# Attention and a gated FFN on one core: first sums of w_out in the upper half of g_3, the last stage's PSUM tile in two, its loads in another order

## The chip, the cores and the metric

One core of a Trainium2 chip runs the whole program. The metric is device microseconds of one execution: the median of 3 runs before is 824.8 us (823.79 to 825.0). Engines: TensorE (PE) multiplies, VectorE (DVE) and ScalarE (ACT) work elementwise, GpSimd (POOL) adds and issues some DMAs, SyncE (SP) issues the other DMAs in the order of its queue. Each engine runs its own instructions in order and waits on counts of the others.

## The reference

```python
scores = scale * np.matmul(q_c, k_c.transpose(0, 1, 2, 4, 3))      # chunks of 64 tokens, 8 x 8 heads, float32
scores = scores - np.max(scores, axis=-1, keepdims=True)
attn = np.exp(scores); attn = attn / (np.sum(attn, axis=-1, keepdims=True) + 1e-09)
out = np.matmul(attn, v_c)
x = out as (4608 tokens, 512)
h = x @ w_in                                                       # 512 x 2048
g = h * (1.0 / (1.0 + np.exp(-1.702 * h)))
return (g @ w_out).astype(np.float32)                              # 2048 x 512
```

## The kernel before

Every float32 factor is split into a high and a low part that TensorE takes at full rate, and a product is three matmuls: high times low, high times high, low times high. The 4608 tokens are 9 blocks of 512. Blocks 0 to 2 are computed plainly. Blocks 3 to 8 go in three pairs (s = 0, 1, 2): `x @ w_in` of a pair is done for eight pairs p of slices of the hidden dimension, each by seven products P1, P2, P6, P7, P5, P3, P4 (i = 0 to 6, `product`, L858 to L860) of sums of quarters of x and of w_in, in place of eight. DVE and ACT drain the seven product banks (`drain`, L839 and L871) into four words per p.

The stage that matters here is the last pair, s = 2, and its `g @ w_out`, which `plan_last` also does by seven products, in the order P4, P1, P2, P6, P7, P5, P3 (L1101 to L1112, PSUM tiles `pl` and `att_last`). Its steps that the change touches:

- **Sums of w_out.** For each p, `plan_tsum` lets POOL add the high and low part of two slices of w_out (`whole`, L991, two instructions) and form four differences (L996 to L999). ACT makes the high part (`th`, L1003), DVE the low part in place (L1006), SP writes both to DRAM (`tsum`, L1010: touth, toutl). The sums alternate between two buffers: even p in `t_a` (tag sA, which later holds the words `kept_6`), odd p in `t_raw`. Sums p may overwrite a buffer only when toutl of p - 2 has landed.
- **x of the last pair.** `plan_x` subtracts quarters of x (L695) and writes high and low parts (L703 on ACT, L706 on DVE). Attention output of the tile pairs 28, 30, 32 and 34 is staged as `xs` in sA, in the half `xe3b` of the tile `g_3`, and in two temporary tiles. `g_3` is 4 x 512 words per partition; `xe3b` is its upper half. The last of these conversions reads the seventh difference, which stands in the second 512 words of `xe3b`.
- **PSUM.** Banks are four `po`, two `hp` and two of the tile `att_last` (L1167: one tile of 2 x 512). In the last pair the products of p take the banks of `turn` in rotation, att0 and att1 among them. Here each of these products and its drain wait on counts that the recording layer derives from the tiles they touch.
- **Loads.** `t_load` (L1063) brings the sums back: those of P4 into a ring of six pieces (the ring that `seven` loads of w_in sums used before), of P6 into w_8 to w_11, of P7 into w_12 to w_15, all through SP.

Which instruction comes when is set by `Plan`: steps with needs, takes, gives and a rank. `ORDER` lists the order by name up to the middle of the second pair; after it, a step goes when its engine is free, its needs are met and its rank is lowest; `NUDGE` shifts single ranks. The plan sets only the order in each queue. On the chip an instruction starts when its counts are reached.

Of the kernel before, what the change touches and what calls it, by code (L numbers as in the profile page):

```python
# [313 lines left out]
def tile_chunk_attention_ffn(  # L314
# [14 lines left out]
    P = 128  # L329
# [42 lines left out]
    }  # L372
    SHIFT = {10: 3.5, 8: 2.0, 26: -12.5, 12: 4.0, 34: -12.5, 6: 3.0}
# [4 lines left out]
    more = ctx.enter_context(tc.tile_pool(name="more", bufs=NTMP))  # L378
    ps_o = ctx.enter_context(tc.tile_pool(name="ps_o", bufs=1, space=bass.MemoryType.PSUM))
    ps_h = ctx.enter_context(tc.tile_pool(name="ps_h", bufs=2, space=bass.MemoryType.PSUM))  # L380
    ps_a = ctx.enter_context(tc.tile_pool(name="ps_a", bufs=1, space=bass.MemoryType.PSUM))

    ident = const.tile([P, P + 96], F32, tag="ident", name="ident")[:, :P]
    make_identity(nc, ident)
# [443 lines left out]
    def plan_two(s, p):  # L828
# [20 lines left out]
        def product(k, i):  # L849
            if bank(i) == "hp":  # L850
                hp = ps_h.tile([P, BT], F32, tag="hp", name=f"hp_{s}_{p}_{i}")
            else:
                hp = held["att"][:, int(bank(i)[3])] if bank(i)[0] == "a" else ps_o.tile([P, DM], F32, tag=bank(i), name=f"hp_{s}_{p}_{i}")
            st[i] = hp
            w = piece(k).rearrange("p (w c f) -> p w c f", w=2, c=2)
            xh, xl = [x_two(OPERANDS[names[i]][1], hl) for hl in range(2)]
            for c in range(2):
                nc.tensor.matmul(hp, w[:, 0, c], xl[:, c], start=c == 0, stop=False)  # L858
                nc.tensor.matmul(hp, w[:, 0, c], xh[:, c], start=False, stop=False)  # L859
                nc.tensor.matmul(hp, w[:, 1, c], xh[:, c], start=False, stop=c == 1)  # L860
# [51 lines left out]
        for i, name in enumerate(names):  # L912
            k = (7 * (NF // 2 * s + p) + i) % 6
            at = rank + STEP * i / 7
            plan.bulk(0.72, at - LEAD, lambda k=k, i=i: load(k, i), need=[f"po_{p}"], make=e(f"ld{i}"), take=[f"piece{k}"])
            xneed = [f"l{OPERANDS[name][1]}x_{s}_{h}" for h in range(2)] if p == 0 else []
            if final and i == 1 and p == 0:
                xneed.append(f"xs_{NTL - 1}")
            before = e(names[i - 1]) if i else h_event(START[s] - 1) if p == 0 else f"{names[6]}_{s}_{p - 1}"
            plan.add(  # L920
                PE, 1.36, at - 0.2, lambda k=k, i=i: product(k, i), need=[e(f"ld{i}"), before] + xneed, make=e(name),
                take=[bank(i)], give=[f"piece{k}"],
            )
            need, take = [e(name)], []
            if i in (1, 2, 3):
                need += [e("d0")] if i == 1 else [e(f"d{i - 1}")]
            if i == 4:
                need += [e("d3")]
                if end:
                    take = ["tmp"]  # L930
                elif final and p == NF // 2 - 1:
                    need += [f"l{x}x_{s}_{h}" for x in range(7) for h in range(2)]
                elif s:
                    need += [f"gl_{g1 - 2 * NF + h}" for h in range(2)]
                else:
                    need += [f"gal_{p // 2}"] + ([f"{x}_0_{h}" for x in ("l6x", "l3x", "t2x", "l5x", "t4x") for h in range(2)] if p > 3 else [])
            if i == 5:
                need += [e("d4")]
            if i == 6:
                need += [e("d4")]  # L940
            if i in (0, 3):
                take = ["tmp"]
            if final and i in (1, 6):
                need += [f"kept_{p}"]
            plan.add(
                ACT if i == 0 else DVE, 0.58 if i == 0 else 1.38 if i == 4 else 0.69, rank - 6 + 0.1 * i, lambda i=i: drain(i),
                need=need, make=e(f"d{i}"), take=take, give=[bank(i)] + ["tmp"] * (final and i in (4, 6)),
            )
# [35 lines left out]
    def plan_tsum(p):  # L984
        st = {}

        def whole(u):
            if u == 0:
                st["x"] = held["t", p % 2]
            w = wt[2 * p + u][:, 1].bitcast(F32)  # L990
            nc.gpsimd.tensor_tensor(st["x"][:, 512 * u : 512 * u + 512], w[:, 0], w[:, 1], op=ALU.add)  # L991

# [19 lines left out]
        rank = START[TWOS - 2] + T_FROM + T_STEP * p  # L1012
        e = lambda a: f"{a}_{p}"
        after = ["tA", "kept_5", (lambda i: f"{('P1', 'P2', 'P6', 'P7', 'P5', 'P3', 'P4')[i % 7]}_{TWOS - 1}_{i // 7}")(T_FIRST + T_EVERY * p)] + ([f"toutl_{p - 2}"] if p > 1 else []) + ([f"tsm_{p - 1}"] if p else [])
        plan.add(POOL, 1.27, rank, lambda: whole(0), need=after, make=e("tw0"))
        plan.add(POOL, 1.27, rank, lambda: whole(1), need=[e("tw0")], make=e("tw1"))
        plan.add(POOL, 3.4, rank, sums, need=[e("tw1")], make=e("tsm"))
        plan.add(ACT, 1.02, rank, hi, need=[e("tsm")] + ([f"touth_{p - 1}"] if p else []), make=e("th"), take=["tmp"])
        plan.add(DVE, 1.23, rank, lo, port=True, need=[e("th")], make=e("tl"))
# [4 lines left out]
    def plan_last():  # L1024
# [36 lines left out]
        def t_load(name, p):  # L1061
            k = T_AT[name]
            nc.sync.dma_start(t_slot(name, p).bitcast(F32), tsum[p, :, 512 * k : 512 * k + 512])  # L1063
# [25 lines left out]
        def o_pe(name, ps, ts):  # L1089
            k = PR.index(name)  # L1090
            if ps[0] == 0:
                if k % 2 == 0:
                    ps_t[k] = [ps_o.tile([P, DM], F32, tag=f"po{t}", name=f"pl_{k}_{t}") for t in range(TB)]
                else:
                    ps_t[k] = [ps_h.tile([P, BT], F32, tag="hp", name=f"pl_{k}_{t}") for t in range(2)]
                    ps_t[k] += [held["att"][:, t] for t in range(2)]
            for t in ts:
                for p in ps:
                    g, c = pair_t[name, p], slice(t * P, t * P + P)
# [51 lines left out]
        def t_tiles(odd):  # L1151
            if odd:
                t = const.tile([P, 4, BT], F32, tag="raw", name="t_raw")
                kept_tiles[5] = lambda h: t[:, h]
                held["t", 1] = t[:, 2:].rearrange("p h t -> p (h t)")
            else:
                t = const.tile([P, 1024], F32, tag="sA", name="t_a")
                kept_tiles[6] = lambda h: t[:, 512 * h : 512 * h + 512]
                held["t", 0] = t

        plan.add(None, 0, -1000, lambda: t_tiles(1), make="kept_5", need=[f"tq1_{NTL - 2}"], take=["raw"])
        plan.add(None, 0, -1000, lambda: t_tiles(0), make="tA", need=[f"l{x}x_{s}_{h}" for x in range(7) for h in range(2)], take=["sA"])
        plan.add(None, 0, -1000, None, make="kept_6", need=["toutl_6"])
        for i in range(NPAIR):
            plan.add(None, 0, -1000, None, need=[f"{PRODUCT_OF[(0, 1, 5)[i // 2]]}_{s}_{NF // 2 - 1}"], give=[f"pb{i}"])

        def att_tile():  # L1167
            held["att"] = ps_a.tile([P, 2, 512], F32, tag="att", name="att_last")

        plan.add(None, 0, -1000, att_tile, need=att_done, take=["att", "att"], give=["att0", "att1"])  # L1170
        last = [f"{n}_{s}_{NF // 2 - 1}" for n in OPERANDS]
# [1 line left out]
        for k, name in enumerate(PR):  # L1173
            before_pe = []
            for p in range(NF // 2):
# [12 lines left out]
                if name in T_AT:  # L1188
                    free = {"P4": [], "P5": [f"ol_P6_{p // 2 * 2 + i}" for i in range(2)]}.get(name, last)
                    plan.add(  # L1190
                        DMA, (1, 0.8, 256), rank - 12, lambda name=name, p=p: t_load(name, p), need=free + [f"touth_{p}", f"toutl_{p}"],
                        make=e("tld"), take=[f"piece{last_k(p)}"] if name == "P4" else [],
                    )
                    need.append(e("tld"))
# [569 lines left out]
```

## Time and profile before

| what | value |
|---|---|
| median of 3 runs | 824.8 us (823.79 to 825.0) |
| the profiled execution | 821.45 us |
| its span, first to last instruction | 819.4 us |
| PE busy | 806.2 us, 98% of the span |
| DVE, ACT, POOL busy | 594.6, 392.1, 187.5 us |
| mean granted clock of TensorE | 0.998 |

The span leaves 2.05 us of the profiled execution outside. PE is the bound: 95% of the chain that ended last is PE. So the time can fall only by the stretches in which PE waits or runs at a lower clock, or if its work gets less. Times in the rows are microseconds from the start of the span; a row of a merged group gives the start of the first and the time to the end of the last. Matmuls are pipelined, so the distance from start to start tells more than the duration of one.

### The profile page before, as it was taken

What the parts mean: (1) busy time and instruction counts of PE and PEld (TensorE: products, weight loads), DVE (VectorE), ACT (ScalarE), POOL (GpSimd) and SP (SyncE); (2) the same over time, 40 slices, a digit from 0 to 9 for tenths busy, and PEclk for the clock granted to TensorE, in tenths of its full rate; (3) what the DMA queues carried; (4) which work ended last, traced back from release to release, by engine and by line L of the source; (5) the groups of instructions that cost most, each with busy time, mean ns of one, the idle gap of its engine ahead of it and who ended that gap; (6) DMA issues with size and microseconds to landing.
All of it is one profiled execution on the core that took longest, in us unless ns stands there. A gap on an engine that the chain in (4) does not pass through costs nothing.

```text
span 819.4 us, 15466 instructions
## 1 busy us (share of the span) xinstructions
PE 806.2 (98%) x5878; PEld 673.4 (82%) x5878; DVE 594.6 (73%) x833; ACT 392.1 (48%) x581; POOL 187.5 (23%) x208
## 2 busy tenths in 40 slices
PE   7999999999999999999999999999999999999998
PEld 6888888888888888888888888888887787888898
DVE  5869976564576869874959874858579667778895
ACT  5989844432544546423435434424353333444542
POOL 1000362211266412020203030200024368300000
PEclk9999999999999999999999999999999999999999
DMA  9996855432485456855765255655440477987221
GB/s 236 345 335 172 273 151 130 84 64 36 85 269 142 108 152 215 186 125 171 169 159 141 49 105 166 158 144 138 127 142 14 139 243 215 304 255 243 60 90 58
DMA packets 233961, 131.06 MB, mean 160 GB/s; under 512 B 173536, under 2 KB 206560, under 8 KB 233888
## 3 DMA queue, kind: packets, MB, share of 16 engines
q1 hardware_dynamic: 230016, 122.08, 54.3%
q0 software_dynamic: 3872, 8.00, 3.1%
q8 instruction: 46, 0.75, 0.4%
q14 instruction: 27, 0.22, 0.1%
HBM read 97.52 MB, written 32.51 MB: 159 GB/s over the span
## 4 chain that ended last, share of the span: by engine, by line
PE 95%; DVE 2%; ACT 1%; DMA 1%; issue 0%; POOL 0%; SPq 0%; DVEq 0%
PE po L1620 13%; PE po L1621 12%; PE po L1622 12%; PE hp L858 8%; PE hp L859 8%; PE hp L860 8%; PE hp L1585 5%; PE hp L1583 5%; PE hp L1584 5%; PE pl L1106 4%; PE pl L1101 2%; PE s L1348 2%; PE x L1422 2%; PE att_last L858 1%; PE att_last L860 1%; PE att_last L859 1%
## 5 line engine op out<-in xcount | busy, mean ns | idle before, releaser
L1620 PE MATMUL po<-w,g_l 128*128 128x512 f32 x448 | 177.1, 395 | 2.9 <-DVE g_l L907 2.5
L1622 PE MATMUL po<-w,g_h 128*128 128x512 f32 x448 | 175.0, 391 | 0.0
L1621 PE MATMUL po<-w,g_h 128*128 128x512 f32 x448 | 175.0, 391 | 0.0
L1620 PEld LDWEIGHTS po<-w,g_l 128*128 128x128 f32 x448 | 84.3, 188 | 21.5 <-DVE g_l L907 2.9
L1622 PEld LDWEIGHTS po<-w,g_h 128*128 128x128 f32 x448 | 84.4, 188 | 17.8
L1621 PEld LDWEIGHTS po<-w,g_h 128*128 128x128 f32 x448 | 84.4, 188 | 16.8
L1397 DVE STREAM_TRANSPOSE eT<-e 32x512 f32<-32x512 f32 x120 | 84.2, 701 | 5.1 <-POOL e L1378 3.2
L858 PE MATMUL hp<-w,w 128*128 128x512 f32 x196 | 76.5, 390 | 0.0
L859 PE MATMUL hp<-w,w 128*128 128x512 f32 x196 | 76.4, 390 | 0.0
L860 PE MATMUL hp<-w,w 128*128 128x512 f32 x196 | 76.3, 389 | 0.0
L898 ACT ACTIVATE g<-g 128x512 f32<-128x512 f32 x48 | 29.9, 630 | 95.1 <-DVE g L839 94.5
L1583 PE MATMUL hp<-x_l,w 128*128 128x512 f32 x184 | 71.8, 390 | 0.0
L1585 PE MATMUL hp<-x_h,w 128*128 128x512 f32 x184 | 71.7, 390 | 0.0
L1584 PE MATMUL hp<-x_h,w 128*128 128x512 f32 x184 | 71.6, 389 | 0.0
L1289 POOL DMA_DIRECT2D raw<-in_k_dram x44 | 26.3, 600 | 152.8 <-DMA v<-in_v_dram 81.4
L1610 DVE TENSOR_TENSOR g_l<-hp,g_h 128x512 fp32r<-128x512 f32 (+1 forms) x50 | 33.1, 663 | 37.4 <-ACT g_h L1605 37.1
L1332 DVE STREAM_TRANSPOSE qkT<-raw 128x1024 f32<-128x1024 f32 x30 | 36.9, 1237 | 27.0 <-PE s L1348 16.2
L1378 POOL TENSOR_TENSOR e<-e,r 128x1024 f32<-128x1024 f32 x16 | 31.3, 1956 | 103.6 <-DVE r L1375 98.8
L1605 ACT ACTIVATE g_h<-hp 128x512 fp32r<-128x512 f32 (+1 forms) x50 | 29.1, 583 | 42.9 <-PE po L1622 41.9
L1604 ACT ACTIVATE hp<-hp 128x512 f32<-128x512 f32 (+1 forms) x50 | 28.4, 569 | 42.9 <-PE hp L1585 32.8
L1639 POOL DMA_DIRECT2D out_dram<-ob x25 | 14.0, 562 | 137.0 <-DVE ob L1634 108.3
L858 PEld LDWEIGHTS hp<-w,w 128*128 128x128 f32 x196 | 36.9, 188 | 7.9 <-ACT d L871 0.2
(222 smaller groups left out, 1716.0 us busy)
## 6 DMA issues: line engine op xcount, KB each, us to landing
w<-seven SPq DMA_DIRECT2D x112, 256.0 KB, 3.0
pieces<-seven SPq DMA_DIRECT2D x56, 256.0 KB, 3.0
seven<-w SPq DMA_DIRECT2D x24, 512.0 KB, 4.0
raw<-in_moe_w_in_dram SPq DMA_DIRECT2D x16, 512.0 KB, 7.2
raw<-in_moe_w_out_dram SPq DMA_DIRECT2D x16, 512.0 KB, 6.9
w<-tsum SPq DMA_DIRECT2D x28, 256.0 KB, 5.0
raw<-in_q_dram SPq DMA_DIRECT2D x208, 32.0 KB, 2.2
v<-in_v_dram SPq DMA_DIRECT2D x26, 256.0 KB, 3.3
```

The costliest lines, as they stand in the source:

```text
L858: nc.tensor.matmul(hp, w[:, 0, c], xl[:, c], start=c == 0, stop=False)
L859: nc.tensor.matmul(hp, w[:, 0, c], xh[:, c], start=False, stop=False)
L860: nc.tensor.matmul(hp, w[:, 1, c], xh[:, c], start=False, stop=c == 1)
L1332: nc.vector.transpose(st["tr"][:, i].rearrange("p n (t j) -> p (n t) j", j=32), st["raw"][:, i].rearrange("p n t j -> p (n t) j"),)
L1397: nc.vector.transpose(st["et"][po : po + 32, :, 32 * a : 32 * a + 32], st["e"][pi : pi + 32, :, 32 * b : 32 * b + 32],)
L1583: nc.tensor.matmul(hp, wh, xl, start=cc == 0, stop=False)
L1584: nc.tensor.matmul(hp, wh, xh, start=False, stop=False)
L1585: nc.tensor.matmul(hp, wl, xh, start=False, stop=cc == NCC - 1)
L1610: nc.vector.tensor_tensor(gl[:, c], hp, gh[:, c].bitcast(F32), op=ALU.subtract)
L1620: nc.tensor.matmul(po, gl[:, c], w[:, 0, :], start=first, stop=False)
L1621: nc.tensor.matmul(po, gh[:, c], w[:, 0, :], start=False, stop=False)
L1622: nc.tensor.matmul(po, gh[:, c], w[:, 1, :], start=False, stop=last)
```

## The change

- `held["t", 0]`, the buffer of the sums of even p, is no longer a tile of its own with tag sA but the upper half `xe3b` of `g_3`. `kept_6` gets the tile with tag sA to itself. The words of p = 7, which are written into that upper half later, need `toutl_6` in the plan now.
- `whole(1)`, which writes the second 512 words, comes ahead of `whole(0)`.
- `att_last` becomes two tiles of one bank each, `att_last_0` and `att_last_1`, in a pool that is opened anew when the attention's PSUM pool is closed.
- The loads of P7 and P6 need the load of P4 for p = 7 (`tld_P4_7`), and two entries of `NUDGE` for loads of P7 go.

```diff
@@ NUDGE
-        "t4x_2_0": -14, "o_97_0": 8, "tld_P7_1": -8, "tld_P7_5": -7, "t3x_2_0": 8, "o_109_2": -3,
+        "t4x_2_0": -14, "o_97_0": 8, "t3x_2_0": 8, "o_109_2": -3,
@@ pools
-    ps_a = ctx.enter_context(tc.tile_pool(name="ps_a", bufs=1, space=bass.MemoryType.PSUM))
+    att_pool = ctx.enter_context(ExitStack())
+    ps_a = att_pool.enter_context(tc.tile_pool(name="ps_a", bufs=1, space=bass.MemoryType.PSUM))
@@ product
-                hp = held["att"][:, int(bank(i)[3])] if bank(i)[0] == "a" else ps_o.tile([P, DM], F32, tag=bank(i), name=f"hp_{s}_{p}_{i}")
+                hp = held["att"][int(bank(i)[3])] if bank(i)[0] == "a" else ps_o.tile([P, DM], F32, tag=bank(i), name=f"hp_{s}_{p}_{i}")
@@ plan_two
-                    need += [f"l{x}x_{s}_{h}" for x in range(7) for h in range(2)]
+                    need += [f"l{x}x_{s}_{h}" for x in range(7) for h in range(2)] + ["toutl_6"]
@@ plan_tsum
-            if u == 0:
-                st["x"] = held["t", p % 2]
+            st["x"] = held["t", p % 2]
...
-        plan.add(POOL, 1.27, rank, lambda: whole(0), need=after, make=e("tw0"))
-        plan.add(POOL, 1.27, rank, lambda: whole(1), need=[e("tw0")], make=e("tw1"))
+        plan.add(POOL, 1.27, rank, lambda: whole(1), need=after, make=e("tw0"))
+        plan.add(POOL, 1.27, rank, lambda: whole(0), need=[e("tw0")], make=e("tw1"))
@@ plan_last
-                    ps_t[k] += [held["att"][:, t] for t in range(2)]
+                    ps_t[k] += [held["att"][t] for t in range(2)]
...
-                t = const.tile([P, 1024], F32, tag="sA", name="t_a")
-                kept_tiles[6] = lambda h: t[:, 512 * h : 512 * h + 512]
-                held["t", 0] = t
+                held["t", 0] = stage_tile("xe3b", "t_a")
+
+        def kept_six():
+            t = const.tile([P, 1024], F32, tag="sA", name="kept_6")
+            kept_tiles[6] = lambda h: t[:, 512 * h : 512 * h + 512]
...
-        plan.add(None, 0, -1000, lambda: t_tiles(0), make="tA", need=[f"l{x}x_{s}_{h}" for x in range(7) for h in range(2)], take=["sA"])
-        plan.add(None, 0, -1000, None, make="kept_6", need=["toutl_6"])
+        plan.add(None, 0, -1000, lambda: t_tiles(0), make="tA", need=[f"l{x}x_{s}_{h}" for x in range(7) for h in range(2)], take=["xe3b"])
+        plan.add(None, 0, -1000, kept_six, make="kept_6", need=[f"l{x}x_{s}_{h}" for x in range(7) for h in range(2)], take=["sA"])
...
-            held["att"] = ps_a.tile([P, 2, 512], F32, tag="att", name="att_last")
+            att_pool.close()
+            ps_l = att_pool.enter_context(tc.tile_pool(name="ps_l", bufs=1, space=bass.MemoryType.PSUM))
+            held["att"] = [ps_l.tile([P, 512], F32, tag=f"att{i}", name=f"att_last_{i}") for i in range(2)]
...
-                        DMA, (1, 0.8, 256), rank - 12, lambda name=name, p=p: t_load(name, p), need=free + [f"touth_{p}", f"toutl_{p}"],
+                        DMA, (1, 0.8, 256), rank - 12, lambda name=name, p=p: t_load(name, p), need=free + [f"touth_{p}", f"toutl_{p}"] + ["tld_P4_7"] * (name in ("P6", "P7")),
```

On POOL, at the end of the sums of p = 0 and the start of those of p = 1 and 2, the order before is this (w_0, w_1, ... are the slices of w_out, `t_a` and `t_raw` the two buffers):

```order
L998 TENSOR_TENSOR t_a_6563<-t_a_6563 128x256
L999 TENSOR_TENSOR t_a_6563<-t_a_6563 128x256
L991 TENSOR_TENSOR t_raw_5808<-w_2_531 128x512
L991 TENSOR_TENSOR t_raw_5808<-w_3_544 128x512
L996 TENSOR_TENSOR t_raw_5808<-t_raw_5808 128x256
L997 TENSOR_TENSOR t_raw_5808<-t_raw_5808 128x256
L998 TENSOR_TENSOR t_raw_5808<-t_raw_5808 128x256
L999 TENSOR_TENSOR t_raw_5808<-t_raw_5808 128x256
L991 TENSOR_TENSOR t_a_6563<-w_4_584 128x512
```

Here the slice of even number comes first (w_2, then w_3). The same place on POOL after the change:

```order
L998 TENSOR_TENSOR g_3_2398<-g_3_2398 128x256
L999 TENSOR_TENSOR g_3_2398<-g_3_2398 128x256
L991 TENSOR_TENSOR t_raw_5808<-w_3_544 128x512
L991 TENSOR_TENSOR t_raw_5808<-w_2_531 128x512
L996 TENSOR_TENSOR t_raw_5808<-t_raw_5808 128x256
L997 TENSOR_TENSOR t_raw_5808<-t_raw_5808 128x256
L998 TENSOR_TENSOR t_raw_5808<-t_raw_5808 128x256
L999 TENSOR_TENSOR t_raw_5808<-t_raw_5808 128x256
L991 TENSOR_TENSOR g_3_2398<-w_5_645 128x512
```

Only the two L991 of each p have changed places, and the even buffer has another name. What the first L991 of p = 0 waits for is another matter: before, for the last L706 of the tile pairs 28 and 32 on DVE, the last reader of sA; now for the last L706 of all, `w_15<-g_3,w_14`, which reads the second 512 words of `xe3b`.

On SP, at the loads of the sums for the last seven products (P4 goes to pieces, w_0 and w_1; P6 to w_8 to w_11; P7 to w_12 to w_15), the order before is this:

```order
L1063 DMA pieces_2555<-tsum_80 128x512 x2
L1063 DMA w_0_329<-tsum_80 128x512 x2
L1063 DMA w_1_441<-tsum_80 128x512 x2
L1063 DMA w_12_1032<-tsum_80 128x512
L1063 DMA w_8_820<-tsum_80 128x512
L1063 DMA pieces_2555<-tsum_80 128x512
L1063 DMA w_8_820<-tsum_80 128x512
L1063 DMA w_14_1150<-tsum_80 128x512
L1063 DMA pieces_2555<-tsum_80 128x512
L1063 DMA w_9_878<-tsum_80 128x512 x2
```

Here four loads to w_12, w_8 and w_14 stand ahead of the last load to pieces. The same place on SP after the change:

```order
L1063 DMA pieces_2555<-tsum_80 128x512 x2
L1063 DMA w_0_329<-tsum_80 128x512 x2
L1063 DMA w_1_441<-tsum_80 128x512 x2
L1063 DMA pieces_2555<-tsum_80 128x512 x2
L1063 DMA w_8_820<-tsum_80 128x512 x2
L1063 DMA w_9_878<-tsum_80 128x512 x2
```

Four loads of 256 KB, two of P6 and two of P7, have moved from ahead of the last P4 load to behind it. On PE, DVE and ACT every instruction stands where it stood.

## Rows read from the trace of the kernel before

**Rows 1.** The page, busy time of each engine.
```profile
PE 806.2 (98%) x5878; PEld 673.4 (82%) x5878; DVE 594.6 (73%) x833; ACT 392.1 (48%) x581; POOL 187.5 (23%) x208
```
**Rows 2.** Waits of PE over the run: us in total, times, longest.
```profile
PE po L1620 <- DVE g_l L907: 2.5, 1, 2.5
...
PE pl L1101 <- DVE g L1067: 0.7, 1, 0.7
...
PE att_last L858 <- DVE g L839: 0.5, 1, 0.5
```
**Rows 3.** Windows: us, busy PE, PEld, DVE, ACT, POOL, clock, DMA.
```profile
633.00:636.00 3.00, 0.49 (x4) 0.07 (x2) 3.00 (x4) 0.63 (x1) 2.77 (x4) 1.00 0.00 0
636.00:639.50 3.50, 3.50 (x9) 2.76 (x10) 3.50 (x3) 1.91 (x2) 3.50 (x3) 0.51 0.00 0
639.50:660.00 20.50, 20.50 (x92) 16.93 (x91) 11.87 (x16) 6.81 (x10) 4.96 (x6) 1.00 0.66 193
```
**Rows 4.** Timeline of PE at its longest wait: start, us, what.
```profile
633.07 0.39 PE L1622 MATMUL po<-w,g_h 128*128 128x512 f32 x1
635.97 0.78 PE L1620 MATMUL po<-w,g_l 128*128 128x512 f32 x1 [2.51 <-DVE g_l L907]
...
639.49 0.40 PE L860 MATMUL hp<-w,w 128*128 128x512 f32 x1
```
**Rows 5.** Timeline of DVE, 625 to 643.
```profile
625.41 1.29 DVE L706 TENSOR_TENSOR w<-xs,w 128x512 fp32r<-128x512 f32 x2
...
629.41 1.41 DVE L907 TENSOR_TENSOR g_l<-g,g_h 128x512 fp32r<-128x512 f32 x1 [0.29 <-ACT g_h L903]
630.73 2.92 DVE L706 TENSOR_TENSOR w<-xs,w 128x512 fp32r<-128x512 f32 x2
...
634.70 1.21 DVE L907 TENSOR_TENSOR g_l<-g,g_h 128x512 fp32r<-128x512 f32 x1
...
642.02 0.69 DVE L839 TENSOR_TENSOR d<-hp,d 128x512 f32<-128x512 f32 x1 [0.69 <-PE hp L860]
```
**Rows 6.** Timeline of ACT, 631 to 657.
```profile
631.52 0.63 ACT L903 ACTIVATE g_h<-g 128x512 fp32r<-128x512 f32 x1 [1.63 <-PE po L1622]
...
650.05 1.05 ACT L1003 ACTIVATE th<-t_a 128x1024 fp32r<-128x1024 f32 x1
...
655.43 1.04 ACT L1003 ACTIVATE th<-t_raw 128x1024 fp32r<-128x1024 f32 x1
```
**Rows 7.** Timeline of POOL, 614 to 662.
```profile
626.86 5.10 POOL L991 TENSOR_TENSOR t_a<-w 128x512 f32<-128x512 f32 x2 [12.05 <-ACT g_h L903]
...
636.46 3.41 POOL L991 TENSOR_TENSOR t_raw<-w 128x512 f32<-128x512 f32 x2
...
641.93 0.74 POOL L998 TENSOR_TENSOR t_raw<-t_raw 128x256 f32<-128x256 f32 x1
...
658.80 2.93 POOL L991 TENSOR_TENSOR t_a<-w 128x512 f32<-128x512 f32 x2 [15.30 <-DMA tsum<-t_a]
```
**Rows 8.** Timeline of PE at two products into att_last.
```profile
695.31 0.39 PE L860 MATMUL hp<-w,pieces 128*128 128x512 f32 x1
696.16 0.50 PE L858 MATMUL att_last<-w,pieces 128*128 128x512 f32 x1 [0.46 <-DVE g L839]
...
734.16 0.39 PE L860 MATMUL hp<-w,w 128*128 128x512 f32 x1
734.57 0.50 PE L858 MATMUL att_last<-w,w 128*128 128x512 f32 x1
```
**Rows 9.** Timeline of PE at the last step of P4.
```profile
745.72 0.39 PE L1106 MATMUL pl<-pieces,w 128*128 128x512 f32 x1
746.78 0.36 PE L1101 MATMUL pl<-pieces,w 128*128 128x256 f32 x1 [0.67 <-DVE g L1067]
```
**Rows 10.** Timeline of SP: issue of the last P4 load.
```profile
739.07 0.35 SPq L1063 DMA_DIRECT2D pieces<-tsum  x1
```
**Rows 11.** Tile pieces, 727 to 750: time from issue to landing of its four loads.
```profile
DMA to landing us min/median/max: 3.4/4.3/7.6
```

## The prediction

> **What bounds the kernel.** I read the busy times first: PE works 98% of the span [rows 1], so only PE's waits can be saved. The waits of PE over the run then name the places [rows 2]: apart from the start-up there are three of 0.5 to 2.5 us, and all three lie in the last pair of blocks. Windows around the longest show something more: in 633 to 636 PE does four matmuls, and in the 3.5 us after it the granted clock is 0.51, the lower of its two levels (1.2 against 2.4 GHz); then it is 1.00 again [rows 3]. The step of a 128x512 matmul at full clock comes from the last of these windows: 20.50 us for 92 of them, 0.22 us, and 0.23 from start to start.
>
> Next the timelines of the engines around that place. PE waits for a low part g_l of DVE that ends at 634.70 + 1.21 = 635.91 [rows 4, 5]. DVE is late because from 629.41 on each of its operations takes about twice as long: 1.41 for an L907, 2.92 for two L706, where two L706 took 1.29 just before [rows 5]. In the same stretch POOL makes its first sums, from 626.86 [rows 7]. Each of these DVE operations reads two operands from SBUF, and POOL's additions do so too.
>
> **First part: sums of p = 0 in the upper half of g_3, second words first.** The first L991 now has to wait for the last L706, since that one reads the words which `whole(1)` overwrites, and `whole(1)` goes first. So no POOL addition can stand beside any of the conversions. What is late next? ACT makes the g_h that this g_l needs at 631.52 + 0.63 = 632.15, after a wait for PE that the change doesn't touch [rows 6]. DVE, without POOL: L907 from 629.41 at some 0.65 a piece (1.29 for two), two L706, one L695, so it is free at about 632.0 and begins g_l at 632.2; that ends at 632.9. PE wants it one step after 633.07, at 633.30 [rows 4]. So PE doesn't wait, with 0.4 us to spare, and the clock, which fell only after this gap, has no reason to fall. Saved: 635.97 - 633.30 = 2.67 us of waiting, and from 635.97 to 639.49, 3.52 us for eight steps where 8 x 0.23 = 1.84 would do, 1.68 us [rows 4]. Together **4.35 us**.
>
> What it adds: after g_l DVE has an L695 and two L706 left with an ACT copy of 0.6 between, so the last L706 ends near 635.0, and POOL begins there and not at 626.86, 8.1 us later, while PE's later work comes 4.35 us sooner. Queued behind on POOL are only sums. Who waits for them is `th` of p = 0 on ACT, which began at 650.05 and now has its turn at 645.7, and `th` of p = 1, 655.43 and now 651.1 [rows 6]. The first six additions took 636.46 - 626.86 = 9.60 us beside a busy DVE [rows 7]; I take that as the upper end, and 5.9 us as the lower (2.93 for a pair [rows 7], four at 0.74). The first sums are then ready at 640.9 to 644.6, before their turn in either case. The second are ready at 646.8 to 654.2, against a turn at 651.1: from 4.3 us to spare to 3.1 us late. Which end? DVE's work there is drains L839 with one operand in PSUM, and such a one took 0.69 next to an addition that took 0.74 at the same time [rows 5, 7]: neither slowed. So I take the lower end, nothing lost. From p = 2 on the sums wait for the landing of earlier sums, and POOL had 15.30 us of idle time there [rows 7], which takes up a start that is 8 us later.
>
> On this the Trainium skill has a rule, in SBUF — State Buffer, section Who interferes with whom: a DVE instruction with two SBUF inputs contends with a GpSimd instruction that reads SBUF, one with a single SBUF input does not, and the loser blocks. The doubled L706 and the undisturbed L839 are what it says; by it the new place costs only the one operation among the drains with both operands in SBUF, which PE doesn't wait for.
>
> The words `kept_6` have sA to themselves, so they no longer wait for the landing of the sums; the words of p = 7 do, but these come seven products later, 42 steps of 0.23 or 9.7 us. Nothing either way.
>
> **Second part: two PSUM tiles of a bank each.** PE's order is the same. Waits change: with one tile, the last product of a p that went into one bank waited for the drain of the fifth product out of the other. That is what the two rows show: at 696.16 PE starts an att_last product released by a DVE drain, 0.85 us after the matmul before it, and at 734.57 the same with 0.41 [rows 8]. With 0.23 a step, **0.62 and 0.18 us** go. The price that could come is that the drains fall behind. At 696 DVE is done with its two drains before the product in question ends, so the banks of the next products are free. DVE's own false waits (a drain held until a product in the other bank was done) go too, which can only let drains start sooner; I count nothing for it. Bounds: nothing to 0.80.
>
> **Third part: loads.** At 746.78 the last step of P4 starts 1.06 us after the matmul before it, where 0.23 would do: 0.83 us [rows 9]. The row names a DVE subtraction, but DVE's part for this step was long done; PE also waits for the last P4 load. That was issued at 739.07 [rows 10], and the slowest of the four loads into pieces took 7.6 us [rows 11]: 746.67, the moment at which PE goes on. The quickest took 3.4. Its issue waits for PE to free a piece and stays where it is, but four loads of 256 KB now come behind it, not ahead. At 3.4 it lands at 742.5, and anything under 6.88 lands before 745.95, when PE wants it. So **0.83 us** goes. The other end is nothing: sixteen loads are issued right behind it, and if all that are under way share the engines, it lands no sooner. I take the gain, because of four equal loads the median took 4.3 and the last, with the others ahead of it, the longest. P6's two moved loads now stand behind one P4 load, P7's two behind all of P6 as well; but P1 and P2 are multiplied ahead of P6, and P6 ahead of P7, at least 8 x 4 x 0.23 = 7.4 us each, so no one waits.
>
> The Trainium skill, DMA: Bandwidth & Descriptors, section Queues, rings and completion order, says that each DMA engine takes the descriptors of a ring in order, though a later one may finish first. By that rule the gain is whole; if landing went by the number under way, it would be nothing.
>
> **Sum.** 4.35 + 0.62 + 0.18 + 0.83 = 5.98 us. Of the profiled execution, 821.45 us, that leaves 815.5 us. The median of the runs shown, 824.8 us, is 3.35 us above that execution. A run can differ by so much without PE's waits being others, so I take the sum off the median: **818.8 us**.
>
> **Rivals.**
> 1. *The contention moves along.* If POOL's sums run at the slow end, the second ones last to 654.2 and meet the g_l that PE needs next, and `th` is 3.1 us late on ACT with further g_h behind it. PE then loses about that: 818.8 + 3.1 = 821.9 us. For it: the first sums did need 9.60 us. Against it: the drains with a PSUM operand beside POOL [rows 5, 7].
> 2. *The doubled DVE times aren't POOL's doing*, and the long wait stays. Only 0.62 + 0.18 + 0.83 = 1.63 us go: 823.2 us. For it: POOL ran from 626.86 and DVE slowed only from 629.41. Against it: in those 2.5 us DVE had no gap, and slowed just after the first one, of 0.29 us [rows 5].
> 3. *The parts don't free what they name*: the banks' waits are real, the load lands as late, and another operation holds g_l. No change, 824.8 us. Against it: the released instruction and the moment agree in each of the places.
> 4. *Slower: the sums become the pace of the stage.* SP issues the stores of the sums ahead of w_in loads in one queue. If the start at 635.0 is passed on in full, each store, and every load behind it, comes 8.1 us late, and PE runs out of w_in sums once, for 8.1 us: 824.8 - 5.98 + 8.1 = 826.9 us. It decides from the point at which the sums are later than the turn of `th`, by more than 6 us at p = 1. For it: one queue. Against it: 15.30 us of idle POOL [rows 7] and up to 4.3 us to spare.
> 5. *The load alone doesn't come sooner*: 818.8 + 0.83 = 819.6 us; it lies within the forecast's own range.
>
> **How the numbers follow.** Forecast with rival 5: 0.72; rival 1: 0.10; rival 2: 0.08; rival 3: 0.05; rival 4: 0.05. A measurement of this kernel tells a difference of about 0.2%, 1.65 us, from none, so faster begins below 823.15. The forecast counts as faster, rival 1 to eight tenths, rival 2 to one half: 0.72 + 0.08 + 0.04 = 0.84. Same: 0.02 + 0.04 + 0.05 = 0.11. Slower: 0.05. The low end is 815.6: the profiled execution less the sum, as fast as the runs go. The high end is 822.4, which takes in rival 1 and leaves out most of rivals 2 to 4.
>
> **What would show it.** In the profile after: no wait of PE of 2.5 us near 633 and no window with a clock near 0.5 after it; L706 and L907 at 0.65 to 0.7 up to the last conversion; POOL's first L991 behind that, near 635; no wait before att_last L858; the last step of P4 without a gap, its load landing in under 6 us. I am wrong if DVE still needs 1.4 us for an L907 with POOL idle, if `th` waits for POOL at p = 0 or 1, or if SP waits at a store of the sums with loads behind it.

## The result, and the profile after

| | before | after |
|---|---|---|
| median | 824.29 us (6 runs, 821.38 to 826.51) | 816.2 us (6 runs, 815.23 to 818.07) |
| ratio | | 0.9905, 95% interval 0.9883 to 0.9927 |
| the profiled execution | 821.45 us, span 819.4 | 816.14 us, span 814.4 |

The change takes 7.8 us off (6.0 to 9.6). Forecast were 818.8 us with 815.6 to 822.4, so the direction and the range held, and the gain was about 2 us larger than the 5.98 of the sum. In the profiled pair it is 6.4 us (below), near the sum. Where the other 1 to 2 us come from is what the experiments are for. In the code after, lines from L380 to about L985 stand 1 later and lines from about L1160 on 4 later; those between stand where they stood.

The busy times on the page, as in [rows 1]: PE lost 1.7 us of them, and its share rose.
```profile
PE 804.5 (99%) x5878; PEld 672.7 (83%) x5878; DVE 589.6 (72%) x833; ACT 391.7 (48%) x581; POOL 182.2 (22%) x208
```
The waits of PE over the run, as in [rows 2] (us in total, times, longest):
```profile
PE x L614 <- ACT first_b L605: 2.6, 2, 1.5
...
PE hp L1587 <- DVE g_l L1614: 0.6, 1, 0.6
PE po L1624 <- DVE g_l L1614: 0.5, 1, 0.5
```
All three waits of [rows 2] are gone. What is left belongs to the start-up and to earlier blocks. The first two windows of [rows 3], at the same times:
```profile
633.00:636.00 3.00, 3.00 (x15) 2.49 (x14) 2.62 (x5) 2.14 (x4) 0.00 (x0) 1.00 0.00 0
636.00:639.50 3.50, 3.50 (x18) 2.88 (x17) 1.48 (x3) 1.48 (x2) 2.99 (x3) 1.00 0.20 36
```
PE does 15 and 18 matmuls where it did 4 and 9, and the clock stays at 1.00. In the first window POOL does nothing now. The timeline of DVE, for [rows 5]:
```profile
630.81 0.69 DVE L908 TENSOR_TENSOR g_l<-g,g_h 128x512 fp32r<-128x512 f32 x1 [0.30 <-ACT g_h L904]
631.42 1.28 DVE L707 TENSOR_TENSOR w<-xs,w 128x512 fp32r<-128x512 f32 x2
...
633.59 0.69 DVE L908 TENSOR_TENSOR g_l<-g,g_h 128x512 fp32r<-128x512 f32 x1 [0.28 <-ACT g_h L904]
...
635.58 0.69 DVE L707 TENSOR_TENSOR w<-g,w 128x512 fp32r<-128x512 f32 x1
...
638.99 0.69 DVE L840 TENSOR_TENSOR d<-hp,d 128x512 f32<-128x512 f32 x1 [0.67 <-PE hp L861]
...
644.46 0.82 DVE L911 TENSOR_TENSOR g<-kept,g 128x512 f32<-128x512 f32 x1 [0.70 <-ACT g L899]
```
A g_l takes 0.69 us where [rows 5] had 1.41 and 1.21, two conversions 1.28 where they had 2.92. The timeline of POOL, for [rows 7]:
```profile
636.43 2.53 POOL L991 TENSOR_TENSOR g<-w 128x512 f32<-128x512 f32 x2 [20.21 <-DVE w L707]
...
642.18 2.54 POOL L991 TENSOR_TENSOR t_raw<-w 128x512 f32<-128x512 f32 x2
...
647.59 0.74 POOL L999 TENSOR_TENSOR t_raw<-t_raw 128x256 f32<-128x256 f32 x1
655.96 2.54 POOL L991 TENSOR_TENSOR g<-w 128x512 f32<-128x512 f32 x2 [7.63 <-DMA tsum<-g]
```
POOL waits for the last conversion (635.58), begins 9.6 us later than before, and is then quicker: 2.53 for two additions, where they took 5.10 and 3.41. Beside it DVE's drains with one operand in PSUM stay at 0.69; the one operation with both operands in SBUF, at 644.46, takes 0.82, and nobody waits for it. The timeline of ACT, for [rows 6]:
```profile
647.02 1.05 ACT L1003 ACTIVATE th<-g 128x1024 fp32r<-128x1024 f32 x1
...
652.40 1.05 ACT L1003 ACTIVATE th<-t_raw 128x1024 fp32r<-128x1024 f32 x1
...
671.47 1.06 ACT L1003 ACTIVATE th<-t_raw 128x1024 fp32r<-128x1024 f32 x1 [1.87 <-POOL t_raw L999]
```
The first two `th` wait for nothing; that of p = 3 waits 1.87 us for POOL, and no wait of PE follows from it. PE at the two products of [rows 8]:
```profile
692.28 0.39 PE L861 MATMUL hp<-w,pieces 128*128 128x512 f32 x1
692.51 0.39 PE L859 MATMUL att_last<-w,pieces 128*128 128x512 f32 x1
...
730.36 0.39 PE L861 MATMUL hp<-w,w 128*128 128x512 f32 x1
730.59 0.39 PE L859 MATMUL att_last<-w,w 128*128 128x512 f32 x1
```
Both steps are 0.23 us, where they were 0.85 and 0.41. The step behind each of the two products has shrunk too, from 0.34 to 0.23; this line of before goes with [rows 8]:
```profile
696.49 0.39 PE L859 MATMUL att_last<-w,pieces 128*128 128x512 f32 x1
```
SP at the last two loads of P4, for [rows 10], and the landing of the four loads into pieces, for [rows 11]:
```profile
733.54 1.73 SPq L1063 DMA_DIRECT2D pieces<-tsum  x2
```
```profile
DMA to landing us min/median/max: 3.2/3.3/3.7
```
The second of the two is issued some 0.3 us ahead of the end of its row, at 734.95, and lands by 738.65. PE's first matmul on it, a step that has no gap now (compare [rows 9]), begins at 741.83, 6.88 us behind the issue, as before:
```profile
741.83 0.28 PE L1101 MATMUL pl<-pieces,w 128*128 128x256 f32 x1
```

**How the traces are compared.** Executions differ by some 1 to 4 us before the stage begins. So each is measured from one instruction, PE's first po matmul behind the last group of x matmuls (its step is 0.34 us and it stands near 626), to the end of the span. That stretch was 819.4 - 625.00 = 194.40 us before and 814.4 - 626.41 = 187.99 us after: 6.41 us less. All 13 traces have the same 5878 matmuls in the same order, so one part of the stretch can be set side by side as well: from that po matmul to the hp matmul ahead of the first product into att_last [rows 8]. It was 695.31 - 625.00 = 70.31 us before and 692.28 - 626.41 = 65.87 after. What a trace has above 65.87 was lost beside the sums. The runs, in the order of their stretch:

| kernel | from, us | span, us | stretch, us | waits for g_l beside the sums | lost beside the sums, us | clock of 0.50 there, us | last P4 load, issue to landing |
|---|---|---|---|---|---|---|---|
| after, again | 625.58 | 813.5 | 187.92 | none | 0.00 | 0 | 4.1 |
| after | 626.41 | 814.4 | 187.99 | none | 0.00 | 0 | 3.7 |
| old halves | 628.67 | 816.7 | 188.03 | none | 0.09 | 0 | 4.2 |
| wait alone | 626.62 | 815.7 | 189.08 | none | 0.00 | 0 | 6.5 |
| sums alone | 627.14 | 816.3 | 189.16 | none | 0.00 | 0 | 6.8 |
| no reads | 626.37 | 816.8 | 190.43 | 0.6 | 1.39 | 0 | 6.3 |
| before | 625.00 | 819.4 | 194.40 | 2.5 | 4.44 | 3.4 | 7.6 |
| more ahead | 626.83 | 821.6 | 194.77 | none | 0.00 | 0 | 6.8 |
| loads alone | 626.39 | 822.3 | 195.91 | 4.6 in three | 7.02 | 3.4 | 4.7 |
| without sums | 627.37 | 823.4 | 196.03 | 4.6 in three | 8.10 | 6.8 | 4.6 |
| before, third | 626.26 | 822.5 | 196.24 | 4.6 in three | 7.13 | 3.4 | 6.8 |
| banks alone | 625.58 | 822.4 | 196.82 | 4.6 in three | 8.16 | 6.8 | 7.4 |
| before, again | 626.27 | 823.3 | 197.03 | 4.6 in three | 6.84 | 3.4 | 7.8 |

The landing is the longest of the four loads into pieces. The last column but one is how long the granted clock stood at 0.50 in the stage's first 25 us.

### The profile page after: what moved, and what is told of

It is laid out like the page before. It is cut to its first block, busy times and chain, and to the rows that moved or that the text cites. A ratio compares the mean times of both kernels' runs of the same rounds, so it can differ in the third digit from the quotient of the medians.

```text
span 814.4 us, 15488 instructions
## 1 busy us (share of the span) xinstructions
PE 804.5 (99%) x5878; PEld 672.7 (83%) x5878; DVE 589.6 (72%) x833; ACT 391.7 (48%) x581; POOL 182.2 (22%) x208
## 4 chain that ended last, share of the span: by engine, by line
PE 96%; ACT 1%; DVE 1%; DMA 1%; SPq 1%; issue 0%; POOL 0%; DVEq 0%
PE po L1624 13%; PE po L1625 12%; PE po L1626 12%; PE hp L859 8%; PE hp L860 8%; PE hp L861 8%; PE hp L1589 5%; PE hp L1587 5%; PE hp L1588 5%; PE pl L1106 4%; PE pl L1101 3%; PE s L1352 2%; PE x L1426 2%; PE att_last L860 1%; PE att_last L859 1%; PE att_last L861 1%
## 5 line engine op out<-in xcount | busy, mean ns | idle before, releaser
L1101 PE MATMUL pl<-w,w 128*128 128x256 f32 x156 | 43.5, 281 | 0.0
```

The lines of the kernel that those rows point to most:

```text
L1101: low = lambda: nc.tensor.matmul(bank[:, :256], g[:, 1, c], right(name, p, 0), start=first and name not in BOTH, stop=False)
```

## The experiments

Times are set against runs of the kernel before on the same chip: 823.88 us (29 runs) for the first four experiments, 823.48 us (17 runs) for the next four.

### The first part alone
On the kernel before:
```diff
...
-        plan.add(POOL, 1.27, rank, lambda: whole(0), need=after, make=e("tw0"))
...
+        plan.add(POOL, 1.27, rank, lambda: whole(1), need=after, make=e("tw0"))
...
-                held["t", 0] = t
+                held["t", 0] = stage_tile("xe3b", "t_a")
...
```


> The first part alone, put on the kernel before: sums of even p in the upper half of g_3, second words first. Theory (POOL's sums beside the conversions are what makes DVE late): POOL's first L991 starts near 635, DVE's L706 and L907 there take 0.65 to 0.7 us, the wait of 2.5 us and the stretch at a clock of 0.51 go, the other two waits of PE (0.5 at att_last, 0.7 at the last step of P4) stay: 4.35 us off, and about 1.6 us above the whole change. Rival 2 (DVE's doubled times are not POOL's doing): the L907 still take 1.2 to 1.4 us and PE still waits 2.5; no change.

Measured: 818.27 us, ratio 0.9924 (0.9896 to 0.9951), 6.3 us off (4.0 to 8.6). POOL begins at 637.16, every L907 up to there takes 0.68 or 0.69, the waits for g_l are gone, and the one ahead of att_last stays:
```profile
PE att_last L858 <- DVE g L839: 0.5, 1, 0.5
```
So the mechanism is the one predicted, and rival 2 falls. The gain reads larger than 4.35, though its interval still takes that in. One thing isn't as expected: the wait at the last step of P4 is all but gone too (a step of 0.31 us), though the loads stand in the old order. The load landed after 6.8 us, just inside the 6.88 that PE leaves it.

### The second part alone
```diff
...
-            held["att"] = ps_a.tile([P, 2, 512], F32, tag="att", name="att_last")
...
+            held["att"] = [ps_l.tile([P, 512], F32, tag=f"att{i}", name=f"att_last_{i}") for i in range(2)]
...
```


> The second part alone, put on the kernel before: att_last as two tiles of one bank. Theory: the steps of 0.85 and 0.41 us ahead of a product into att_last become 0.23, 0.80 us off in the trace, the 2.5 us wait and the 0.7 us wait stay. Rival 3 (the wait is for the product's own bank and not for the other): the steps stay at 0.85 and 0.41, nothing off. A time cannot tell 0.8 us from none here, the steps in the trace can.

Measured: 823.27 us, ratio 0.9988 (0.9971 to 1.0005). The time can't tell it from none. PE at the two products:
```profile
699.61 0.39 PE L861 MATMUL hp<-w,pieces 128*128 128x512 f32 x1
699.83 0.39 PE L859 MATMUL att_last<-w,pieces 128*128 128x512 f32 x1
...
737.69 0.39 PE L861 MATMUL hp<-w,w 128*128 128x512 f32 x1
737.91 0.39 PE L859 MATMUL att_last<-w,w 128*128 128x512 f32 x1
```
Both steps are 0.22 us, so the waits were for the other bank and go with the tile. The long wait isn't 2.5 us here, though:
```profile
PE po L1623 <- DVE g_l L908: 4.6, 3, 3.3
...
PE pl L1102 <- DMA pieces<-tsum: 0.5, 1, 0.5
```
Three waits of PE for g_l instead of one, 4.6 us in all. This was expected by neither theory. The clock stays low longer, too: 6.83 us at 0.50 (windows as in [rows 3]), where before had some 3.4. So this stretch isn't shorter than that of before, though the two steps are.
```profile
638.10:644.93 6.83, 5.69 (x13) 4.51 (x14) 4.66 (x5) 1.99 (x3) 4.85 (x5) 0.50 0.00 0
```

### The third part alone
```diff
-        ... "tld_P7_1": -8, "tld_P7_5": -7, ...
...
-  need=free + [f"touth_{p}", f"toutl_{p}"],
+  need=free + [f"touth_{p}", f"toutl_{p}"] + ["tld_P4_7"] * (name in ("P6", "P7")),
```


> The third part alone, put on the kernel before: loads of P6 and P7 behind the last load of P4. Theory: that load takes 3.4 to 6 us to land, the last step of P4 has no gap (1.06 becomes 0.23 us), 0.83 us off; the other waits stay. Rival 5 (loads under way share the engines, whatever their order): its landing still takes about 7.6 us with sixteen loads behind it, and PE still waits 0.7 us.

Measured: 824.16 us, ratio 1.0001 (0.9986 to 1.0016). The load lands within 4.7 us with sixteen loads behind it, and the last step of P4 has no gap: both against rival 5. The time shows none of it. Its waits for g_l are the three of 4.6 us as well, although this kernel is the same as before up to the loads, 100 us later.

### The change without its first part
The diffs of the second and third part together.

> The whole change without its first part. Theory: the wait of 2.5 us near 633 and the clock of 0.51 behind it are there as before, the other two waits are gone: 0.80 + 0.83 = 1.6 us off the kernel before, 4.35 us above the whole change. Rival 3 (the small parts free nothing): as the kernel before.

Measured: 823.97 us, ratio 0.9989 (0.9973 to 1.0006), 0.9 us off where 1.6 was forecast (between 2.2 off and 0.5 more). The small waits are gone, the stall stands, again with 4.6 us in three waits. Beside the 0.9905 of the whole change, the first part is what moves the time.

### A wait alone
```diff
             if u == 0:
                 st["x"] = held["t", p % 2]
+            if u == 0 and p == 0:
+                z = x_two(6, 1).bitcast(F32)[:, 1, 510:512]
+                nc.gpsimd.tensor_tensor(st["x"][:, :2], z, z, op=ALU.add)
```


> The kernel before, with one addition of 2 words of the last converted slice (w_15) put on POOL ahead of its first sum, so that POOL waits for the last L706; no tile, bank or load is moved. Theory (only the time at which POOL starts matters): POOL starts near 636, no wait of PE near 633, and the time is that of the first part alone, 5 to 7 us off (818.3 us against 823.9 there). Rival (the buffer matters: the sums stand in sA as before, or the halves are in the old order, and something else holds DVE): the wait stays, nothing off, or a late th costs 3 us of it.

Measured: 818.14 us, ratio 0.9935 (0.9921 to 0.995), 5.3 us off (4.1 to 6.5), inside the interval of the first part alone (4.0 to 8.6), and its stretch of 189.08 stands beside 189.16. POOL's start, which the two words hold back:
```profile
636.58 0.18 POOL L992 TENSOR_TENSOR t_a<-w 128x2 f32<-128x2 f32 x1 [20.15 <-DVE w L706]
636.84 2.54 POOL L994 TENSOR_TENSOR t_a<-w 128x512 f32<-128x512 f32 x2
```
So neither the buffer nor the order of the halves saves time by itself. When POOL starts does.

### No reads on POOL
```diff
+            if p == 0:
+                for _ in range(3):
+                    nc.gpsimd.memset(st["x"][:, 512 * u : 512 * u + 512], 0.25)
+                return
...
```


> The kernel before, with POOL's additions for p = 0 replaced by operations that only write: three memsets of 512 words for each of the two L991 and eight of 256 words for the four differences. It leaves out the sums of p = 0. Theory (what holds DVE is that both it and POOL read two operands of SBUF): beside the memsets L706 and L907 take 0.65 to 0.7 us, and the first wait of PE goes; the additions of p = 1 come behind them and may still meet the last conversions, for at most the 2.5 to 3.3 us that the longest wait takes. Rival (any POOL work on SBUF slows DVE): L907 at 1.2 to 1.8 us as soon as POOL starts, and all waits as before.

Measured: 818.77 us, ratio 0.9949 (0.993 to 0.9968), 4.2 us off (2.6 to 5.8). POOL:
```profile
628.19 3.33 POOL L992 MEMSET t_a<- 128x512 f32 x6 [12.02 <-ACT g_h L903]
631.47 2.09 POOL L1002 MEMSET t_a<- 128x256 f32 x8
633.53 2.98 POOL L995 TENSOR_TENSOR t_raw<-w 128x512 f32<-128x512 f32 x2
```
And DVE beside it:
```profile
628.58 0.69 DVE L907 TENSOR_TENSOR g_l<-g,g_h 128x512 fp32r<-128x512 f32 x1
...
631.38 1.29 DVE L706 TENSOR_TENSOR w<-xs,w 128x512 fp32r<-128x512 f32 x2
632.58 0.68 DVE L695 TENSOR_TENSOR xt<-xs 128x512 f32<-128x512 f32 x1
633.55 1.82 DVE L907 TENSOR_TENSOR g_l<-g,g_h 128x512 fp32r<-128x512 f32 x1 [0.28 <-ACT g_h L903]
635.29 1.77 DVE L695 TENSOR_TENSOR g<-g,xt 128x512 f32<-128x512 f32 x1
```
This is the plainest picture of the case. For 5.3 us POOL writes without a pause into the same buffer, and DVE keeps 0.69. At 633.53 POOL's first addition begins, the next g_l takes 1.82, and PE waits 0.6 us for it. So reading matters, and work as such doesn't. The Trainium skill, SBUF — State Buffer, section Who interferes with whom, says just this: a DVE instruction with two SBUF inputs contends with a GpSimd instruction that reads SBUF, and not with one that only writes it.

### The old order of the halves
```diff
-        plan.add(POOL, 1.27, rank, lambda: whole(1), need=after, make=e("tw0"))
-        plan.add(POOL, 1.27, rank, lambda: whole(0), need=[e("tw0")], make=e("tw1"))
+        plan.add(POOL, 1.27, rank, lambda: whole(0), need=after, make=e("tw0"))
+        plan.add(POOL, 1.27, rank, lambda: whole(1), need=[e("tw0")], make=e("tw1"))
```


> The whole change, but with whole(0) ahead of whole(1), as before. Theory (second words first is what holds POOL back until the last conversion): POOL's first addition, of the first 512 words, starts some 6 us sooner, once those words are read, and stands beside two or three of DVE's conversions, at 1.2 to 1.8 us each; then POOL waits for the last one. PE waits 0 to 1.5 us for g_l near 633, so 0 to 2.5 us above the whole change. Rival (the order of the halves doesn't matter): POOL starts where it does with the whole change, no wait of PE, no difference.

Measured: 817.47 us, ratio 0.9926 (0.9909 to 0.9944), which overlaps that of the whole change. The first half goes early, the second late:
```profile
632.33 1.60 POOL L991 TENSOR_TENSOR g<-w 128x512 f32<-128x512 f32 x1 [13.86 <-DVE xs L696]
638.96 1.28 POOL L991 TENSOR_TENSOR g<-w 128x512 f32<-128x512 f32 x1 [5.03 <-DVE w L707]
```
It costs DVE one slow operation, a g_l of 1.41 us, and PE nothing: no wait there, and a stretch of 188.03 against 187.99. So the price lay at the lower end of what was expected; "second words first" wasn't needed in this execution.

### More loads ahead
```diff
+        "tld_P6_0": -20, "tld_P6_1": -20, "tld_P6_2": -20, "tld_P6_3": -20,
+        "tld_P7_0": -20, "tld_P7_1": -20, "tld_P7_2": -20, "tld_P7_3": -20,
-  ... + ["tld_P4_7"] * (name in ("P6", "P7")),
```


> The whole change, but with eight loads of P6 and P7, 256 KB each, ahead of the last two loads of P4 on SP (the kernel before had two and four, the whole change none). Theory (loads land in the order of the queue, and the four of 256 KB ahead were what made 7.6 us of 3.4): the last P4 load is issued 3 to 6 us later than with the whole change and lands behind what is ahead of it, 7 us or more from its issue; PE has 3.1 us to spare there, so it waits 2 to 6 us at the last step or two of P4. Rival 5 (landing goes by the number under way, whatever the order): it lands 3.5 to 4 us from its issue as with sixteen behind it, and PE waits 0 to 2 us.

Measured: 821.44 us, ratio 0.9977 (0.9964 to 0.9991); of the gain some 4 us are lost again, beside the 817.47 of old halves on the same chip. The profiled execution, 823.38 us, is the slowest of the 12 and lost more: its stretch is 6.8 us above that of the whole change. SP issues the last two P4 loads from 738.06 on, where the whole change had 733.54 (in an execution 0.4 us earlier), and the slowest lands 6.8 us from its issue where that had 3.7:
```profile
738.06 0.98 SPq L1064 DMA_DIRECT2D pieces<-tsum  x2
```
PE waits for the first of them until 745.02, and the granted clock is at 0.50 from 743.9, in the end of that wait, to 750.7 (windows as in [rows 3]):
```profile
741.00:745.00 4.00, 0.00 (x0) 0.01 (x1) 3.68 (x6) 0.63 (x1) 0.00 (x0) 0.86 0.98 337
745.00:751.00 6.00, 5.98 (x19) 5.13 (x20) 1.29 (x2) 1.11 (x2) 0.00 (x0) 0.52 0.82 315
```
With 3.7 us of landing it would have come at 741.8, 0.9 us after PE wanted it (740.83, one step behind its last matmul at 740.60); it came at 744.9. So what stands ahead in the queue counts, and sixteen loads behind count for little: the last load landed after 3.7 to 4.7 us with them, against rival 5. It isn't in proportion: with eight ahead the landing took 6.8 us, with the four of the old order 6.3 to 7.8. By the rule of the Trainium skill, DMA: Bandwidth & Descriptors, section Queues, rings and completion order, a ring's descriptors are taken in order; the two landings agree with it.

### Before again, twice, and after again
The kernels as they are.

> The kernel before once more, unchanged, to see whether the size of the stall is its own or that of one execution. Theory (the stall has two sizes, whichever of DVE and POOL goes first): either as in the profile shown (DVE undisturbed up to its first gap, POOL's first two additions 5.1 us, one wait of PE of 2.5 us), or as with the second and third part alone (the first L907 beside POOL at 1.78 us, POOL's two additions 3.3 us, three waits of 0.4, 1.0 and 3.3 us). Rival (the larger stall came with the second and third part): as in the profile shown.

> The kernel before a third time, unchanged. Theory and rival as for the second time; if the large stall is the common one, it is to be seen in at least one of the two.

> The changed kernel once more, unchanged. Theory (no addition of POOL beside a conversion, so nothing there has two sizes): no wait of PE from 610 to the end again, the stretch from PE's last short gap before the stage (the po step of 0.34 us near 605) to the end of the span 209.0 us as before, to within 0.5 us. Rival (the stage scatters for another reason): a wait of PE or a stretch that differs by over 1 us.

Measured, one execution each: 825.37, 824.6 and 815.31 us. Both of before have the larger stall. A run of before beside them, without a profile, took 827.80 us at a mean granted clock of 0.995. PE's waits in the first of them:
```profile
PE po L1620 <- DVE g_l L907: 4.6, 3, 3.3
...
PE pl L1101 <- DMA pieces<-tsum: 0.9, 1, 0.9
```
Its POOL and its DVE where the sums begin:
```profile
628.12 3.29 POOL L991 TENSOR_TENSOR t_a<-w 128x512 f32<-128x512 f32 x2 [12.05 <-ACT g_h L903]
```
```profile
627.89 0.68 DVE L695 TENSOR_TENSOR xt<-xs 128x512 f32<-128x512 f32 x1
628.49 1.78 DVE L907 TENSOR_TENSOR g_l<-g,g_h 128x512 fp32r<-128x512 f32 x1
```
Here POOL's two additions take 3.29 us and DVE is slow at once, at 628.49. In the profile shown first they took 5.10 and DVE was slow 2.5 us later [rows 5, 7], though POOL's first addition (626.86) began at the same point of DVE's work. These two lines of before belong to [rows 5]:
```profile
626.62 0.69 DVE L695 TENSOR_TENSOR xt<-xs 128x512 f32<-128x512 f32 x1
627.22 0.68 DVE L907 TENSOR_TENSOR g_l<-g,g_h 128x512 fp32r<-128x512 f32 x1
```
The changed kernel had no wait there either time: its stretches are 187.99 and 187.92.

So PE's waits in the kernel before have two sizes. Of six traces in which POOL starts as before (before three times, banks alone, loads alone, without sums), five have the large one, 4.6 us in three. The rival, that it came with the other parts, falls. What the stall costs has three sizes in these six, since the stretch at the lower clock differs as well: 4.4 us (waits of 2.5), 6.8 to 7.1 (waits of 4.6, the clock low for 3.4 us) and 8.1 to 8.2 (the same waits, the clock low for 6.8).

## Why the prediction was right, and where its size was off

- **First part, the mechanism: right.** No L991 beside a conversion, g_l at 0.69, no wait of 2.5 us, clock 1.00. Sums alone and wait alone show that POOL's start is the cause; the memsets show that its reads are. Rival 2 is out.
- **First part, the size: right for the profiled execution, too small for the others.** By the matmuls set side by side the stall cost 4.44 us there, against 4.35 forecast. The stretches agree: 194.40 less the 0.83 of the load is 193.57, and sums alone has 189.16: 4.4 us. In the other two of before, by the same two ways, it cost 6.8 and 7.1 us: 196.24 (next to no gap at the load) and 197.03 - 1.08 (its step of 1.31 us there, less 0.23), less the mean of sums alone and wait alone, 189.12, is 7.1 and 6.8. In banks alone and without sums it cost 8.2 and 8.1.
- **What it adds: right, at the lower end.** The changed execution reaches the stage 1.41 us later than before (626.41 against 625.00). With that taken off, POOL starts at 635.0 (forecast 635.0), the first sums are done at 640.8 (640.9) and the second at 646.9 (646.8). No `th` is late at p = 0 or 1. Rival 1 is out, but for 0.13 us of one L911, and so is rival 4: POOL's idle time fell from 15.30 to 7.63 us, and no wait of PE came of it.
- **Second part: right in the trace, a little larger.** Both steps are 0.23 us, in banks alone 0.22. The step behind each fell from 0.34 to 0.23 as well, so the part is worth 0.62 + 0.11 + 0.18 + 0.11 = 1.02 us and not 0.80. From sums alone and wait alone to the whole change the stretch falls by 1.17 and 1.09 us, nearly all of it at these places. The time can't show it, and the stretches of banks alone and without sums hide it behind their larger stall.
- **Third part: the mechanism right, the size not fixed.** PE leaves the load 6.88 us, as worked out. In the old order it landed after 6.3, 6.5, 6.8, 6.8, 7.4, 7.6 and 7.8 us in seven traces, so the gap is there in three of them (0.68, 0.83 and 1.08 us), and in four it is 0.08 us at most. In the new order it landed within 3.7 to 4.7. The term is worth 0 to 1.1 us, and 0.83 was one draw of it. That it came out so in the profiled execution is luck.
- **The step that failed** is the one from the trace to the median: "A run can differ by so much without PE's waits being others." The waits were others. The profile was taken of an execution with the small stall, 821.45 us, near the fastest of its kernel. The two that were profiled again took 825.37 and 824.6, with stretches 2.6 and 1.8 us longer, and they came into the stage 1.3 us later. Subtracting the price of the small stall from a median of runs that, by five of the six traces, have a larger one left 2 us over. With stretches, the gain is 6.4 us from the small one and 8.3 to 9.1 from the other two of before; the runs gave 7.8 (6.0 to 9.6). The range held by its low end, which was taken from the profiled execution (815.6; the sum leaves 815.5): the measured 816.2 lies 0.6 us above it.
- **The scatter goes with the clock, in part.** Of the 29 runs of before beside the first experiments, 12 have a mean granted clock of 1.000, so that it can't have been at the lower level for 1 us in all; their median is 822.9 us. The 13 at 0.997 or 0.998, as the profiled one, have 825.0, and the four at 0.995 or 0.996 have 827.4. Of the 17 runs beside the next experiments four have 1.000. None of the six traces is of this kind, so what PE waits for in such a run isn't known, and neither is which size is the common one. That the stall makes all of the spread is not shown: the start of the program scatters too.

## What to carry to other kernels

Where DVE's operations double in length, look what POOL reads at that moment, and try first to start POOL later: an addition of two words did here what a moved buffer did. A wait that comes out of two engines contending can have more than one size, so profile the kernel before two or three times, compare the mean granted clock of each with that of the unprofiled runs, and don't subtract a price from a median that it wasn't read from, above all if the profiled execution is quicker than the median. A load landed here by what stood ahead of it in its queue; a margin between landing and use that is smaller than the scatter of the landing is a wait in some executions.

## What the runs showed of the hardware that was not expected

- **One phase, two outcomes.** In all six traces with the old start POOL's first addition begins 0.23 or 0.24 us after DVE's L695 begins. Five times POOL needs 3.3 us for two additions (2.53 with no conversion beside them) and DVE's next operation takes 1.78. Once DVE goes through three more operations at 0.68 or 0.69 and POOL takes 5.1. The Trainium skill, SBUF — State Buffer, section Who interferes with whom, says that the order of issue decides who blocks. By the starts in the traces that order is the same here, so it doesn't tell these two apart. What does was not tried.
- **Contended operations mostly come in steps.** In before, again, DVE's 128x512 operations beside POOL's additions take 1.21 to 1.22 or 1.75 to 1.78 us one by one, against 0.68 or 0.69 alone. In other traces values between stand as well: 1.41 in [rows 5] and in old halves, 0.82 after the change.
- **In the last pair the clock fell at the long waits only, and not always at the same point of them.** At the wait of 3.3 us in before, again, the steps of PE's matmuls go from 0.23 to 0.43 us; the granted clock is 0.50, the lower of the two levels, from 0.56 us ahead of the wait's end (639.92), while in before, third, it fell 1.0 us behind the end, and in more loads ahead 1.1 us ahead of it. At the waits of 0.4 and 1.0 us in before, again, no step of 0.43 followed. In the start-up it fell once at shorter ones: sums alone has 0.50 from 28.93 to 32.34, behind waits of 1.1 and 0.9 us.
